# Two layers of experts on one core: another row of step numbers for the last layer-one job's routing

## The chip, the cores and the metric

The kernel runs on one core of a Trainium2 chip. The core has a matrix engine (TensorE, PE in the rows), a vector engine (VectorE, DVE), an activation engine (ScalarE, ACT), a general engine (GpSimd, POOL) and SyncE (SP); each runs its own queue of instructions in order, and semaphores tie the queues together. Sixteen DMA engines move data between memory and the core's buffers; DMAs are issued from the queues of SP, ACT and POOL. The metric is the device time of one execution in microseconds.

## The reference

Three stages follow one another. First, decayed linear attention over 2 x 768 tokens with 8 heads of 64. Its output, 1536 rows of 512, goes to a layer of 8 experts that takes one expert for each token, and the result of that to a second layer of 8 experts that takes two, chosen from logits with noise:

```python
x = attn_out ...reshape(B * S, H * D)          # 1536 x 512
# layer one
gate_w = softmax(normalised x @ expert_emb.T / tau)[argmax]
out[mask] = gate_w * (relu(x[mask] @ w1[e]) @ w2[e])
# layer two
noisy_logits = x @ w_gate + log1p(exp(x @ w_noise)) * noise
top2 = the two largest of noisy_logits, with softmax over the two
out[mask] += top2_w * (relu(x[mask] @ w1[e]) @ w2[e])
```

## The kernel before

The experts' work is cut into 18 jobs, numbered from 0. Jobs 0 to 7 are layer one, one expert each, with up to 224 rows of tokens. Jobs 8 and 9 are the first 256 rows of layer two's experts 0 and 1, job 10 is expert 2 of layer two with up to 416 rows, and jobs 11 to 17 are the rest of layer two. Jobs 8 and 9 run early: the rows of job 8 come from tokens of layer-one jobs 0 to 5, those of job 9 from jobs 0 to 6, those of job 10 from all.

A job has eight steps, one for each 128 columns of the hidden width. A step is: `hstep` (four products with the first weights, in a high and a low part, L751, L752, L756), `ystep` of two steps before (products with the second weights, L795 to L797 in jobs 8 and 9), whatever a table `todo` holds for this job and step, and `split`, which cuts the weights for the step three ahead into parts (ScalarE L348, L349; DVE L350, L352). The schedule is manual: each engine's queue holds its instructions in the order in which the program writes them.

For every layer-one job the result is routed to layer two by ten stages, put into `todo` during the next job. With the job they belong to named j, the numbers of a row such as `WHEN7` are the steps of job j + 1 at which the stages run; 8 and above are steps of job j + 2:

```python
stages = (pe_0, pe_1, post1_a, post1_b, post1_m, post1_h, post1_c, post1_c2, post1_d, post1_e)
when = {0: WHEN0, E - 3: WHEN5, E - 2: WHEN6, E - 1: WHEN7}
after = {E + i: when[E - 3 + i][-1] % NF for i in range(3)}
...
for n in range(NEARLY, E + 1):
    put(n + 1, after[n + 2], window2, n)
for j in range(E, NJ):
    put(j - 1, after.get(j, 0), gather2, j)
```

`pe_0` and `pe_1` make the layer's output rows and the gate products. `post1_a` is the gates' exponential and logarithm on ScalarE (L919, L921). `post1_b` finishes the noisy logits on DVE (L927, L928, and five small operations recorded at L331), `post1_m` finds the two largest and their numbers (L939, L941) and has POOL convert the numbers (L942) and subtract the two values (L943). `post1_h` makes the one-hot rows (DVE L950, POOL L954, L955) and the exponential of the difference (ScalarE L956). `post1_c` and `post1_c2` compute each token's rank in its expert (TensorE L963 to L966, DVE L972 to L987) and write the rows to memory (POOL L992). `post1_d` builds two factors of a table (DVE L999 to L1002), and `post1_e` multiplies them on TensorE (L1010) and adds the product to the table of layer two (DVE L1011).

A table gives a gather its indices: `window2` makes them on DVE (L658, L661), and `gather2` issues one indirect DMA on POOL for each 128 rows (L693). With `WHEN6`, whose last number is 12, the table for job 9 is done in job 8, step 4, and job 9's indices and gather follow in the same step. With `WHEN7` the same holds for job 10 in job 9. The transposes of gathered rows (L732) stand in job 8, step 6 for job 9 and in job 9, steps 6 and 7 for job 10. Results of job 8 go out through DVE L1054 and ScalarE L1052 and a scatter on POOL (L1056).

Within a step the functions run in the order in which they were put, with `post1_e`, `pe_0` and `pe_1` ahead of the others. The stages of the jobs were put ahead of `window2` and `gather2`.

In the profiled execution, steps 4 to 7 of job 8 begin on TensorE at 277.86, 280.90, 283.80 and 287.91 us, steps 0, 1, 6 and 7 of job 9 at 290.88, 293.77, 308.23 and 313.89 us, and job 10 at 319.63 us.

Of the kernel before, what the change touches and what calls it, by code (L numbers as in the profile page):

```python
# [59 lines left out]
WHEN = (2, 3, 3, 5, 6, 7, 9, 10, 11, 13)  # L60
WHEN5 = (2, 3, 3, 3, 5, 6, 7, 8, 9, 11)
WHEN6 = (2, 3, 5, 5, 7, 8, 9, 9, 11, 12)
WHEN7 = (2, 3, 4, 5, 5, 6, 7, 7, 7, 9)
ORDER2 = (0, 1, 2, 5, 3, 6, 4)
XG5 = (5, 6, 6, 4, 5)
XG6 = (6, 6, 6, 8, 8)
# [33 lines left out]
def emit(ctx, tc, qt, kt, k, v, lam, moe_expert_emb, moe_tau, moe_w1, moe_w2, moe2_w_gate, moe2_w_noise,  # L100
# [1094 lines left out]
# [3 lines that stand above are left out]
# [290 lines left out]
```

## Time and profile before

| | |
|---|---|
| median of 3 runs | 599.55 us (598.65 to 602.4) |
| profiled execution | 603.23 us, its span 601.5 us |
| TensorE busy | 577.0 us (96%) |
| DVE busy | 378.5 us (63%) |
| ScalarE busy | 293.6 us (49%) |
| POOL busy | 211.0 us (35%) |
| mean granted clock of TensorE | 0.98 |

The span runs from the first to the last instruction of one execution; the profiled execution's own time lies 1.7 us above it. Busy shares are over the whole span; which engine is late in a stage is read from the waits and the timeline of that stage. The granted clock is told as a share of 2.4 GHz; 0.50 is the lower level, 1.2 GHz.

### The profile page before, as it was taken

To read this page: it belongs to the slowest core of one execution; us is meant where nothing else is said; L and a number is where in the kernel's file an instruction comes from. 1 tells how busy PE (TensorE), PEld (TensorE's weight loads), DVE (VectorE), ACT (ScalarE), POOL (GpSimd) and SP (SyncE) were. 2 spreads that over 40 slices of the span, in tenths; PEclk is the share of its full clock that TensorE was granted. 3 is DMA by queue.
4 is the path that set the end of the run, shared out by engine and by line. 5 is a ranking of instruction groups with operands and counts; after the bars stand their busy time and mean duration, and the time that the engine had idled before them with its cause. 6 is when DMAs were issued, how large, how long until landed. Compare 5 with 4: busy or idle time off the path is not lost. (4 is left out here: it accounts for less than half of the span.)

```text
span 601.5 us, 11485 instructions
## 1 busy us (share of the span) xinstructions
PE 577.0 (96%) x4212; PEld 485.5 (81%) x4213; DVE 378.5 (63%) x1172; ACT 293.6 (49%) x689; POOL 211.0 (35%) x409
## 2 busy tenths in 40 slices
PE   6999989999999999999999999999999999999992
PEld 2899779999999998997767878788888898679761
DVE  3588858688888888888866455465664137324620
ACT  1366536677676766675544343434443135314410
POOL 5486634433524523223362401422303342412103
PEclk8699999999999999999999999999999999999997
DMA  6989737858777765856692734356526647747104
GB/s 204 340 300 373 285 94 253 313 194 282 279 282 266 273 222 189 303 177 198 201 316 103 229 141 145 52 196 171 153 56 160 210 98 235 239 142 192 18 5 57
DMA packets 59954, 119.51 MB, mean 199 GB/s; under 512 B 5469, under 2 KB 7045, under 8 KB 59890
## 3 DMA queue, kind: packets, MB, share of 16 engines
q10 hardware_dynamic: 37232, 73.74, 35.0%
q0 software_dynamic: 9376, 25.48, 16.3%
q1 hardware_dynamic: 13282, 19.48, 9.8%
q8 instruction: 35, 0.57, 0.4%
q14 instruction: 29, 0.24, 0.1%
HBM read 100.55 MB, written 18.14 MB: 197 GB/s over the span
## 5 line engine op out<-in xcount | busy, mean ns | idle before, releaser
L751 PE MATMUL h<-xs,h 128*128 128x224 f32 (+10 forms) x512 | 149.1, 314 | 0.0
L752 PE MATMUL h<-xs,h 128*128 128x224 f32 (+10 forms) x512 | 142.7, 302 | 0.0
L1056 POOL DMA_INDIRECT out_dram<-orow,ix x30 | 48.6, 1620 | 207.7 <-DVE orow L1054 153.4
L350 DVE TENSOR_TENSOR l<-r,h 128x512 bf16<-128x512 f32 x128 | 88.2, 689 | 33.4 <-ACT h L348 31.8
L787 ACT ACTIVATE hs<-h 128x224 fp32r<-128x224 f32 (+10 forms) x128 | 52.0, 406 | 103.4 <-PE h L756 103.0
L756 PEld LDWEIGHTS <-l 128*128 128x128 bf16 x896 | 74.1, 97 | 30.8 <-issue 8.5
L752 PEld LDWEIGHTS h<-xs,h 128*128 128x128 f32 x512 | 97.4, 190 | 1.5 <-DVE xs L737 0.5
L751 PEld LDWEIGHTS h<-xs,h 128*128 128x128 f32 x512 | 97.2, 190 | 1.3
L788 DVE SCALAR_TENSOR_TENSOR hs<-h,hs 128x224 fp32r<-128x224 f32 (+10 forms) x128 | 57.9, 452 | 51.8 <-ACT hs L787 51.5
L756 PE MATMUL h<-xs,l 128*128 128x224 bf16 (+10 forms) x512 | 87.9, 293 | 0.0
L352 DVE TENSOR_TENSOR l<-r,h 128x512 bf16<-128x512 f32 x125 | 85.5, 684 | 0.0
L348 ACT ACTIVATE h<-r 128x512 fp32r<-128x512 f32 x128 | 79.8, 623 | 5.7 <-DVE hs L788 1.9
L349 ACT ACTIVATE h<-r 128x512 fp32r<-128x512 f32 x128 | 79.5, 621 | 0.0
L749 PE MATMUL y<-hs,h 128*128 128x448 f32 (+5 forms) x256 | 64.2, 372 | 0.0
L756 PE MATMUL y<-hs,l 128*128 128x224 bf16 (+8 forms) x384 | 62.5, 284 | 0.0
L737 DVE TENSOR_TENSOR xs<-t,xs 128x416 fp32r<-128x416 f32 (+7 forms) x42 | 24.7, 590 | 55.5 <-ACT xs L736 55.2
L751 PE MATMUL y<-hs,h 128*128 128x416 f32 (+2 forms) x128 | 49.6, 388 | 0.0
L736 ACT ACTIVATE xs<-t 128x416 fp32r<-128x416 f32 (+7 forms) x42 | 21.6, 518 | 54.5 <-PE t L732 51.2
L797 PE MATMUL y<-h,hs 128*128 128x512 f32 x80 | 47.1, 589 | 0.0
L752 PE MATMUL y<-hs,h 128*128 128x416 f32 (+2 forms) x128 | 44.6, 349 | 0.0
L749 PEld LDWEIGHTS y<-hs,h 128*128 128x128 f32 x256 | 42.6, 189 | 0.9
L693 POOL DMA_INDIRECT xw<-x,g x28 | 31.9, 1141 | 18.2 <-PE h L756 7.5
(274 smaller groups left out, 924.5 us busy)
## 6 DMA issues: line engine op xcount, KB each, us to landing
r<-in_moe_w_dram ACTq DMA_DIRECT2D x66, 1024.0 KB, 7.1
r<-in_moe_w_dram SPq DMA_DIRECT2D x6, 1024.0 KB, 9.4
x<-row POOLq DMA_DIRECT2D x8, 517.0 KB, 8.0
out_dram<-zeros ACTq DMA_DIRECT2D x7, 512.0 KB, 6.1
qt<-in_qt_dram SPq DMA_DIRECT2D x12, 256.0 KB, 5.1
kr<-in_k_dram SPq DMA_DIRECT2D x12, 256.0 KB, 5.8
vt<-in_v_dram SPq DMA_DIRECT2D x12, 256.0 KB, 5.8
x<-xr POOLq DMA_DIRECT2D x11, 265.0 KB, 5.0
```

What stands on the lines that cost most here:

```text
L348: nc.scalar.activation(h1, a1, AF.Copy)
L349: nc.scalar.activation(h2, a2, AF.Copy)
L350: nc.vector.tensor_sub(l1, a1, h1.bitcast(FT))
L352: (nc.gpsimd if s < LEAD else nc.vector).tensor_sub(l2, a2, h2.bitcast(FT))
L749: nc.tensor.matmul(o[:, :2 * c], hi, mov, start=first, stop=last, skip_group_check=True)
L751: nc.tensor.matmul(o[:, :c], hi, mov[:, :c], start=first, stop=False, skip_group_check=True)
L752: nc.tensor.matmul(o[:, :c], hi, mov[:, c:], start=False, stop=last, skip_group_check=True)
L756: nc.tensor.matmul(o[:, :c], lo, upper_half(mov[:, :c]), start=first, stop=last, skip_group_check=True)
L787: nc.scalar.activation(hh, ph[:, :c], AF.Relu)
L788: nc.vector.scalar_tensor_tensor(hl, ph[:, :c], 0.0, hh.bitcast(FT), op0=OP.max, op1=OP.subtract)
L797: nc.tensor.matmul(PY[j][t], hl, h2, start=False, stop=f == NF - 1)
L1056: s = nc.gpsimd.indirect_dma_start(out=out[:, :], out_offset=bass.IndirectOffsetOnAxis(ap=ix[:p, t:t + 1], axis=0), in_=row[:p], in_offset ...
```

## The change

One row of step numbers changes, that for job 7, the last of layer one:

```diff
-WHEN7 = (2, 3, 4, 5, 5, 6, 7, 7, 7, 9)
+WHEN7 = (2, 3, 3, 4, 4, 5, 7, 7, 7, 8)
```

`post1_a` goes from step 4 to 3 of job 8, `post1_b` and `post1_m` from 5 to 4, `post1_h` from 6 to 5; `post1_c`, `post1_c2` and `post1_d` stay at step 7. `post1_e` goes from step 1 of job 9 to step 0, and by `after` the indices and the gather for job 10 go with it. The instructions are the same in number and kind; SP's queue does not change.

On DVE in job 8, step 4 (L1011 is the table's sum with job 6, `g` and `ok` are the indices and marks for job 9), the kernel before has:

```order
L1011 TENSOR_TENSOR tab_142<-tab_142,t 128x96
L658 TENSOR_SCALAR g_4705<-tab_142 128x2
L661 TENSOR_SCALAR ok_4706<-tab_142 128x2
L350 TENSOR_TENSOR l_4714<-r_4195,h_4712 128x512
L352 TENSOR_TENSOR l_4715<-r_4197,h_4713 128x512
L788 SCALAR_TENSOR_TENSOR hs<-h,hs 128x256
L927 RECIPROCAL q_4651<-q_4651 128x16
L928 SCALAR_TENSOR_TENSOR q_4651<-q_4651 128x16
```

and the changed kernel:

```order
L1011 TENSOR_TENSOR tab_142<-tab_142,t 128x96
L927 RECIPROCAL q_4651<-q_4651 128x16
L928 SCALAR_TENSOR_TENSOR q_4651<-q_4651 128x16
L331 TENSOR_TENSOR q_4651<-q_4651 128x16 x2
L331 TENSOR_TENSOR q_4651<-q_4651,lg_4650 128x16
L331 TENSOR_TENSOR q_4651<-q_4651,meta 128x16
L331 TENSOR_TENSOR q_4651<-q_4651,lg_4650 128x16
L939 MAX mx_4712<-q_4651 128x8 x2
L941 MAX_INDEX mi_4713<-mx_4712,q_4651 128x8 x2
L658 TENSOR_SCALAR g_4720<-tab_142 128x2
L661 TENSOR_SCALAR ok_4721<-tab_142 128x2
```

The indices for job 9 stand behind the eleven operations of job 7's decisions now; before, those came a step later.

On POOL in job 8, steps 4 and 5 (L693 is the gather for job 9):

```order
 L913 COPY row_4594<-meta 128x2
 L920 TENSOR_SCALAR q_4651<-q_4651 128x16
-L693 DMA xw<-x_69,g_4705 128x517 x2
-L942 CAST row_4594<-mi_4750 128x2x2
-L943 TENSOR_TENSOR q_4651<-mx_4749 128x2
-L954 TENSOR_TENSOR q_4651<-oh_4791 128x16
-L955 TENSOR_TENSOR ob_4794<-q_4651,ok_1352 128x16
+L942 CAST row_4594<-mi_4713 128x2x2
+L943 TENSOR_TENSOR q_4651<-mx_4712 128x2
+L693 DMA xw<-x_69,g_4720 128x517 x2
+L954 TENSOR_TENSOR q_4651<-oh_4757 128x16
+L955 TENSOR_TENSOR ob_4760<-q_4651,ok_1352 128x16
```

The gather for job 9 stands behind the conversion and the subtraction of job 7's decisions.

On POOL in job 9, steps 0 and 1 (L693 is the gather for job 10, L1056 a scatter of job 8's results):

```order
-L1056 DMA out_dram<-orow,ix 1952x512
-L693 DMA xw<-x_69,g_4953 128x517 x3
-L693 DMA xw<-x_69,g_4953 32x517
+L693 DMA xw<-x_69,g_4904 128x517 x3
+L693 DMA xw<-x_69,g_4904 32x517
+L1055 MEMSET spacer 1x1
+L1056 DMA out_dram<-orow,ix 1952x512
```

The gather for job 10 goes ahead of the scatters.

## Rows read from the trace of the kernel before

**Rows 1.** The page, part 1: busy us, share of the span, instructions.
```profile
PE 577.0 (96%) x4212; PEld 485.5 (81%) x4213; DVE 378.5 (63%) x1172; ACT 293.6 (49%) x689; POOL 211.0 (35%) x409
```

**Rows 2.** Waits of TensorE: us in total, times, longest us.
```profile
PE t L732 <- DMA xw<-x,g: 1.3, 4, 0.4
```

**Rows 3.** Timeline, TensorE, 311 to 320 us: start, duration, instruction, idle before.
```profile
311.53 0.30 PE L732 MATMUL t<-ident,xw 128*128 128x128 f32 x1 [0.35 <-DMA xw<-x,g]
...
312.81 1.16 PE L732 MATMUL t<-ident,xw 128*128 128x128 f32 x6 [0.36 <-DMA xw<-x,g]
...
313.89 0.39 PE L751 MATMUL h<-xs,h 128*128 128x256 f32 x1
...
318.38 1.32 PE L732 MATMUL t<-ident,xw 128*128 128x128 f32 x8
...
319.63 0.46 PE L751 MATMUL h<-xs,h 128*128 128x416 f32 x1
```

**Rows 4.** Windows: length, each engine's busy us, clock, DMA share, GB/s.
```profile
316.00:317.00 1.00, 1.00 (x5) 0.60 (x4) 0.62 (x2) 0.39 (x1) 1.00 (x1) 0.50 1.06 414
...
318.00:319.00 1.00, 1.00 (x8) 0.68 (x6) 0.00 (x0) 0.00 (x0) 0.45 (x2) 0.99 1.03 418
```

**Rows 5.** Timeline, POOL, 291 to 304 us.
```profile
291.97 0.81 POOL L992 DMA_DIRECT2D x<-row  x1 [0.30 <-POOL row L991]
...
298.56 1.68 POOL L1056 DMA_INDIRECT out_dram<-orow,ix  x1 [5.41 <-DVE tab L1011]
...
303.52 1.17 POOL L693 DMA_INDIRECT xw<-x,g  x1 [0.31 <-DVE ex L331]
```

**Rows 6.** DMA issues, us to landing: of 303 to 304.5, of 291 to 294.
```profile
xw<-x,g POOLq DMA_INDIRECT x1, 7.9
...
x<-row POOLq DMA_DIRECT2D x1, 517.0 KB, 4.6
```

**Rows 7.** Timeline, TensorE, 283 to 294 us (job 8, steps 6 and 7; job 9).
```profile
283.80 0.28 PE L751 MATMUL h<-xs,h 128*128 128x256 f32 x1
...
286.59 0.27 PE L732 MATMUL t<-ident,xw 128*128 128x128 f32 x1
...
287.18 0.98 PE L732 MATMUL t<-ident,xw 128*128 128x128 f32 x7 [0.31 <-DMA xw<-x,g]
...
287.91 0.37 PE L751 MATMUL h<-xs,h 128*128 128x256 f32 x1
...
293.77 0.28 PE L751 MATMUL h<-xs,h 128*128 128x256 f32 x1
```

**Rows 8.** Timeline, DVE, 281 to 294 us.
```profile
281.48 0.16 DVE L661 TENSOR_SCALAR ok<-tab 128x2 f32<-128x2 f32 x1
...
283.35 0.24 DVE L927 RECIPROCAL q<-q 128x16 f32<-128x16 f32 x1
...
285.13 0.16 DVE L941 FIND_INDEX8 mi<-mx,q 128x8 uint32<-128x8 f32 x1
...
293.17 0.56 DVE L1002 TENSOR_TENSOR pb<-oi,ge 128x384 f16<-128x384 f32 x1
```

**Rows 9.** Timeline, POOL, 281 to 287 us.
```profile
281.86 1.34 POOL L693 DMA_INDIRECT xw<-x,g  x1 [1.05 <-DVE ok L661]
...
283.50 0.97 POOL L693 DMA_INDIRECT xw<-x,g  x1 [0.30 <-issue]
...
285.89 0.64 POOL L943 TENSOR_TENSOR q<-mx 128x2 f32<-128x2 f32 x1
```

**Rows 10.** DMA issues, us to landing: of 283.4 to 284.6, of 313 to 314.2.
```profile
xw<-x,g POOLq DMA_INDIRECT x1, 3.6
...
xw<-x,g2r POOLq DMA_INDIRECT x1, 5.5
```

**Rows 11.** Timeline, ScalarE and its DMA queue, 280 to 286 us.
```profile
280.03 0.21 ACT L919 ACTIVATE q<-q 128x16 f32<-128x16 f32 x1
...
285.40 0.37 ACTq L320 DMA_DIRECT2D r<-in_moe_w_dram  x1
```

## The prediction, made before the changed kernel ran

> **What bounds the kernel now.** I read the page's busy shares first: TensorE is busy 577.0 of 601.5 us [rows 1], so a microsecond counts only if TensorE loses or wins it. The waits of TensorE come next. In the whole stretch that the change touches they hold one entry: the transposes of gathered rows, which waited four times for the gather's DMA, 1.3 us in all [rows 2]. The timeline says where. Three of the four waits stand in job 9, step 6, ahead of the transposes that feed job 10 [rows 3], and one in job 8, step 6, ahead of those that feed job 9 [rows 7]. Nothing else there is late by the profile, so the change can act only through these two gathers, and through what a wait does to TensorE's clock.
>
> The wait for job 10 is dearer than its own idle time. TensorE ended the work before it at 311.53 - 0.35 = 311.18 us and began the next step at 313.89 [rows 3], which is 2.71 us for eight transposes. Seven of them took 287.91 - 287.18 = 0.73 us in job 8 [rows 7], so eight take 0.83 and the wait cost 1.9 us. Then the granted clock fell to its lower level, 1.2 GHz (0.50 of 2.4 GHz), and was back at 0.99 in the slice from 318 us [rows 4]. In that time step 7 took 318.38 - 313.89 = 4.49 us [rows 3] against 286.59 - 283.80 = 2.79 us for a step with the same instructions in job 8 [rows 7], and the second eight transposes took 319.63 - 318.38 = 1.25 us against 0.83. The fallen clock cost 1.7 + 0.4 = 2.1 us. Wait and clock together are **4.0 us**, and this is all that an earlier gather for job 10 can win.
>
> **The change part by part.** No instruction is added or removed. Four things move.
>
> *The table and the gather for job 10 move from step 1 to step 0 of job 9.* The gather's indices are then ready one step, some 3 us, sooner. On POOL's queue the four gathers now stand ahead of the two scatters of job 8's rows. Before, the scatters went first, at 298.56 us, and the first gather was issued at 303.52 [rows 5]. It landed 7.9 us later [rows 6], after the time at which TensorE wanted it. In the changed order the gathers must wait for the rows of the last layer-one job, whose write is issued at 291.97 [rows 5] and lands 4.6 us later [rows 6], at 296.6. The indices follow the table's sum, which came just ahead of 298.56 [rows 5] and now comes a step of 2.8 us sooner, near 295.7. So the gathers start near 297, that is 6 us sooner. Even at 7.9 us the first lands at 305 and the last, some 4 us behind it, at 309. TensorE asks at 311.2: the wait goes, with 2 us to spare, and so does the fall of the clock. Term: **-4.0 us**, bounds -4.0 and 0 (the gathers stay late). What is late next there is the scatters, now issued some 4 us later; nobody waits for them before the next job's scatters. The four table products themselves come on TensorE at 293.77 [rows 7], just where their operand is finished (293.17 + 0.56 = 293.73 [rows 8]): 0 to 0.3 us, taken as 0.1 and left out of the sum.
>
> *The decisions of job 7 (reciprocal to the index search) move from step 5 to step 4 of job 8.* This is where it costs. Step 4 is also the step that builds job 9's indices and issues job 9's gather, and the order shows that the moved work stands ahead of both: on DVE eleven instructions between the table's sum and the indices, on POOL the cast and the subtraction (L942, L943) ahead of the two gathers. On DVE these eleven took from 283.35 to 285.13 + 0.16 = 285.29, 1.94 us [rows 8]. POOL's two need the result of the last of them and ended at 285.89 + 0.64 = 286.53 [rows 9], 1.24 us later; the indices (L658, L661) run beside these. Before, DVE began the indices just ahead of 281.48 [rows 8], at 281.4, and the gathers were issued at 281.86 and 283.50 [rows 9]. Now the first comes at 281.4 + 1.94 + 1.24 + 0.3 for the issue = 284.9 us. To that I add 0.4 us, because ScalarE's two small activations, 0.21 us the first [rows 11], also move a step up and delay the weight split on which DVE waits next: 285.3, that is 3.4 us late (3.0 without it). With the same spacing of 1.64 us the second gather is issued at 286.9.
>
> The second gather of job 9 landed 3.6 us after issue [rows 10], at 287.1, and TensorE already waited 0.31 us for it [rows 7]. There is no slack, so every microsecond is paid. The nearest row for a free queue gives 286.9 + 3.6 = 290.5, +3.4 us. But two weight blocks of 1 MB were issued at 285.40 [rows 11] and come some 0.8 us later in the changed order, so the gather now moves beside them. A gather that was issued into such a load took 5.5 us [rows 10]; one behind two scatters took 7.9 [rows 6]. I take 4.4, nearer to 3.6, since the load starts only about when this gather does: landing at 291.3. Term: **+4.2 us**, bounds +3.0 (no delay from ScalarE, 3.6 us) and 286.9 + 7.9 - 287.1 = +7.7.
>
> The Trainium skill, page "DMA: Bandwidth & Descriptors", section "Queues, rings and completion order", says that each DMA engine goes round the queues that have work, a packet from each in turn. By that rule the gather shares with the weight load and the term stays near +4.2; if it had to stand behind the whole load instead, the term would be near its upper bound. The 5.5 us of rows 10 lean to sharing.
>
> *TensorE's clock after that wait.* TensorE would stand idle, but for one transpose, from 286.59 + 0.27 = 286.9 to 291.3, 4.4 us. In the trace of before a wait spread over 311.18 to 313.89 brought the clock down [rows 3 to 4]; the longer one should too. There is one step, not a second set of transposes, in the slow stretch: **+1.7 us**, bounds 0 (no fall, as after the 0.31 us wait) and 2.6 (a slow stretch half as long again).
>
> *The one-hot rows (step 5) and the gates' exponential.* ScalarE's exponential L956 now waits about 2 us for POOL's late subtraction, with the splits for job 9's first step queued behind it; these are needed some 4 us later. DVE's share runs ahead of a TensorE that is itself late. Cost nothing; if that cover were gone, under 1 us. The ranks stay at step 7, so their chain keeps its place.
>
> **Sum:** -4.0 + 4.2 + 1.7 = +1.9 us. The profiled execution took 603.23 us, its span 601.5 and 1.7 around it, and would become 605.1. The runs shown have a median of 599.55, 3.7 us below that execution; the same addition gives **601.5 us**.
>
> **The rivals.** *A: as summed*, one wait exchanged for a somewhat dearer one, 601.5 us (its own range 599.5 to 604.0). Chance 0.62.
> *B: the wait moves but the clock holds.* Job 9's wait costs 3.0 to 4.2 us and no slow stretch follows: -1.0 to +0.2, about 599.2 us. For it: the one transpose in the middle of the wait, and the chance of where the fall lands. Against: the wait is longer than the one that brought a fall. Chance 0.20.
> *C: only the gain is seen,* -4.0, 595.5 us: the delayed gather is still in time. It needs a gather issued 3 us later to land no later; against it stands the 0.31 us that TensorE waits already. Chance 0.08.
> *D: the gather sinks in the weight load.* It lands at 294.8, +7.7, with the clock's 2.1, less 4.0: +5.8, 605.4 us. It decides from a landing time of about 7.5 us. For it: the 7.9 us row; against: that one stood behind scatters in its own queue. Chance 0.07.
> *E: the change does not do what it says* for job 10: the gathers, now ahead of the scatters, are held until the rows are written and land as late as before. Then +4.2 + 1.7 = +5.9, 605.5 us. Against: the write lands at 296.6 by its row, 14 us ahead of the need. Chance 0.03.
>
> **How the numbers follow.** A measurement of this kernel can tell about 1% from no change, that is 6.0 us: below 593.6 or above 605.5. Neither A, B nor C reaches these; D and E stand at the upper edge. Faster 0.01, slower 0.06, the same 0.93. The range takes in A and B with the bounds of the contention, and the 3.8 us over which the runs of before scatter: 597.0 to 605.0. It leaves out C and the ends of D and E.
>
> **What would show it.** In the changed trace: the first gather for job 9 issued 3.0 to 3.4 us later against the end of the preceding table sum, behind L943; a wait of 3 to 5 us at the transposes in job 8, step 6, and a stretch at 0.50 behind it; the gathers for job 10 ahead of the scatters; job 9, step 6 without a wait and step 7 at 2.8 us. The forecast is wrong if the wait in job 8 is under 2 us, if the clock falls in both places or in neither, or if a third wait turns up, at the table products of job 9, step 0.

## The result, and the profile after

The changed kernel takes 607.02 us (median of 4 runs, 605.68 to 609.43) against 599.63 us before (median of 4, 598.65 to 602.4): 7.4 us more by the medians, ratio 1.0106 with a 95% interval of 1.0075 to 1.0138, which is 4.5 to 8.3 us. The sum had given +1.9 us: the way is right, the size is a third to a quarter of the measured one, and the median lies outside the range. The two places and their signs are as forecast; the sizes of the two main terms are not.

The waits of TensorE in the changed kernel's profile (us in total, times, longest us) answer to [rows 2]:

```profile
PE t L732 <- DMA xw<-x,g: 5.6, 2, 4.5
...
PE y L795 <- DVE key L1142: 0.3, 1, 0.3
```

Four waits of 0.3 to 0.4 us became two, of 4.5 and 1.1 us, and a small new one came. The timeline of TensorE shows where; the first four lines answer to [rows 7], the last four to [rows 3]:

```profile
292.08 0.48 PE L732 MATMUL t<-ident,xw 128*128 128x128 f32 x1 [4.46 <-DMA xw<-x,g]
293.68 1.75 PE L732 MATMUL t<-ident,xw 128*128 128x128 f32 x7 [1.12 <-DMA xw<-x,g]
295.08 0.56 PE L751 MATMUL h<-xs,h 128*128 128x256 f32 x1
...
298.71 0.18 PE L963 MATMUL t<-oacc,ones 128*128 128x16 bf16 x1
...
319.43 1.32 PE L732 MATMUL t<-ident,xw 128*128 128x128 f32 x8
320.67 0.39 PE L751 MATMUL h<-xs,h 128*128 128x256 f32 x1
...
323.56 1.31 PE L732 MATMUL t<-ident,xw 128*128 128x128 f32 x8
324.81 0.46 PE L751 MATMUL h<-xs,h 128*128 128x416 f32 x1
```

Both waits now stand ahead of the transposes for job 9. Ahead of those for job 10 there is none: the eight run as one group, and the next step begins at once. TensorE's clock fell inside the wait, as the windows show (length, busy us of each engine, clock, DMA share, GB/s):

```profile
290.00:291.00 1.00, 0.00 (x0) 0.00 (x0) 0.00 (x0) 0.00 (x0) 0.00 (x0) 0.50 1.08 428
295.00:296.00 1.00, 1.00 (x7) 1.00 (x6) 0.69 (x1) 0.74 (x3) 0.00 (x0) 0.50 0.00 0
297.00:298.00 1.00, 1.00 (x8) 0.76 (x6) 1.00 (x3) 0.59 (x3) 0.00 (x0) 1.00 0.00 0
```

All of the engines but the DMA stand still at 290 us, and DMA moves 428 GB/s. What it moves is told by the queues. On DVE, the decisions of job 7 come first and the indices of job 9 behind them (compare [rows 8]):

```profile
282.30 0.24 DVE L927 RECIPROCAL q<-q 128x16 f32<-128x16 f32 x1
...
284.07 0.16 DVE L941 FIND_INDEX8 mi<-mx,q 128x8 uint32<-128x8 f32 x1
...
284.21 0.16 DVE L661 TENSOR_SCALAR ok<-tab 128x2 f32<-128x2 f32 x1
```

On POOL, the conversion and the subtraction, then the two gathers for job 9; the last two lines are the first gather for job 10 and the first scatter behind it (compare [rows 5, 9]):

```profile
284.30 1.32 POOL L942 CAST row<-mi 128x4 f32<-128x4 uint32 x1 [3.88 <-DVE g L658]
285.59 0.18 POOL L943 TENSOR_TENSOR q<-mx 128x2 f32<-128x2 f32 x1
285.93 1.09 POOL L693 DMA_INDIRECT xw<-x,g  x1 [0.16 <-DVE hs L788]
287.33 1.36 POOL L693 DMA_INDIRECT xw<-x,g  x1 [0.30 <-issue]
...
304.13 1.04 POOL L693 DMA_INDIRECT xw<-x,g  x1 [3.10 <-DVE ws L1034]
...
310.05 1.65 POOL L1056 DMA_INDIRECT out_dram<-orow,ix  x1 [0.23 <-issue]
```

The weight load on ScalarE's queue, two blocks of 1 MB, is issued between the two gathers, 286.26 - 284.65 = 1.6 us after the step's start as before (285.40 - 283.80 [rows 11]); the second block follows 0.4 us later. Its first line:

```profile
286.26 0.38 ACTq L320 DMA_DIRECT2D r<-in_moe_w_dram  x1
```

The two gathers took, from issue to landing, 6.1 and 6.3 us (6.0 to 6.6 in the later traces `a_again` and `decide_only`), where the second took 3.6 before [rows 10]:

```profile
xw<-x,g POOLq DMA_INDIRECT x1, 6.1
...
xw<-x,g POOLq DMA_INDIRECT x1, 6.3
```

To compare executions I use lengths of steps, from the first product of a step to the first of the next on TensorE's timeline. The time of a whole execution also holds the opening of the kernel, where the clock is not the same each time. The stretch from 18 to 20 us shows it, in the profiled execution of before and in one of the runs below, `table_only`, which has the same instructions there:

```profile
18.00:20.00 2.00, 1.66 (x24) 1.47 (x20) 0.45 (x2) 0.60 (x1) 1.98 (x2) 0.50 1.05 385
```

and in table_only:

```profile
18.00:20.00 2.00, 1.13 (x18) 1.14 (x20) 0.91 (x3) 1.19 (x4) 1.93 (x2) 0.98 1.06 389
```

Job 8, step 3 began at 272.85 us in the first and at 270.76 in the second: 2 us apart before anything of the change runs. Over all executions it began between 270.76 and 273.71 us. The steps in us, for all profiled executions of this study ("sum" is from job 8, step 3 to job 10; the steps not listed are the same in all, 10.9 us for 8.3 to 8.5 and 8.4 for 9.3 to 9.5; the last column is the ratio of times to before, with its interval):

| kernel | 8.6 | 8.7 | 9.0 to 9.2 | 9.6 | 9.7 | sum | ratio |
|---|---|---|---|---|---|---|---|
| before | 4.11 | 2.97 | 8.99 | 5.66 | 5.74 | 46.78 | 1 |
| b_again (before) | 4.11 | 2.98 | 9.01 | 5.30 | 4.13 | 44.87 | 1.0006 (0.9982 to 1.003) |
| b_third (before) | 3.93 | 2.96 | 9.01 | 5.39 | 4.16 | 44.79 | |
| b_fourth (before) | 4.02 | 2.98 | 9.01 | 5.32 | 4.16 | 44.83 | |
| after | 10.43 | 3.72 | 9.43 | 4.04 | 4.14 | 51.10 | 1.0106 (1.0075 to 1.0138) |
| a_again (after) | 10.75 | 4.57 | 9.42 | 4.03 | 4.13 | 52.21 | |
| table_only | 3.94 | 2.98 | 9.43 | 4.05 | 4.13 | 43.87 | 0.9978 (0.9954 to 1.0002) |
| decide_only | 10.42 | 4.49 | 8.98 | 5.24 | 4.14 | 52.57 | 1.0159 (1.011 to 1.0208) |
| gather_first | 3.96 | 2.96 | 9.43 | 4.05 | 4.14 | 43.88 | 0.997 (0.9945 to 0.9995) |
| load_late | 7.17 | 4.52 | 9.44 | 4.05 | 4.14 | 48.65 | 1.0078 (1.0051 to 1.0106) |
| pool_split | 6.63 | 4.55 | 9.44 | 4.05 | 4.13 | 48.14 | 1.0046 (1.0019 to 1.0073) |
| filled | 9.84 | 2.96 | 9.42 | 4.03 | 4.14 | 49.70 | 1.0085 (1.0056 to 1.0113) |

The usual sum of before is 44.8 us, that of after 51.1 to 52.2: 6.3 to 7.4 us. From the start of job 10 to the end of the span all twelve executions took 281.4 to 282.2 us, so no part of the difference lies behind job 10, and these 6.3 to 7.4 us are the measured difference within its interval.

### The profile page after: what moved, and what is told of

The parts are those of the page before. It is cut to its first block, busy times and chain, and to the rows that moved or that the text cites. A ratio compares the mean times of both kernels' runs of the same rounds, so it can differ in the third digit from the quotient of the medians.

```text
span 606.2 us, 11486 instructions
## 1 busy us (share of the span) xinstructions
PE 577.4 (95%) x4212; PEld 486.1 (80%) x4213; DVE 378.5 (62%) x1172; ACT 293.3 (48%) x689; POOL 212.7 (35%) x409
## 5 line engine op out<-in xcount | busy, mean ns | idle before, releaser
L1056 POOL DMA_INDIRECT out_dram<-orow,ix x30 | 47.6, 1587 | 205.0 <-DVE orow L1054 155.9
L693 POOL DMA_INDIRECT xw<-x,g x28 | 33.1, 1180 | 20.0 <-PE h L756 7.3
```

Source lines behind the costliest of these rows:

```text
L1056: s = nc.gpsimd.indirect_dma_start(out=out[:, :], out_offset=bass.IndirectOffsetOnAxis(ap=ix[:p, t:t + 1], axis=0), in_=row[:p], in_offset ...
```

## The experiments

My theory after the result: job 9's late gather, landing together with the weight load, is the loss, and what job 10 wins is small. The rivals: the first trace of before was untypical, so that there was nothing like 4 us to win; or the table's own move costs something.

**b_again, b_third, b_fourth.** The kernel before, unchanged.

> The kernel before, unchanged, for a second trace. Theory one (the loss is job 9's late gather; the wait for job 10's gather with the clock's fall, 3.2 us by the traces of before and after, is in the usual run of before): the trace shows TensorE waiting at the transposes of job 9, step 6, and a granted clock of 0.50 behind it, and a time near 599.6 us. Rival, the untypical trace (the profiled execution of before, 603.23 us, had that wait, the usual one of 599.6 us does not): no clock of 0.50 in job 9, step 7, and step 6 to job 10 about 3 us shorter than the 11.4 us of the first trace.

> The kernel before, a third trace, to see how often the clock falls behind job 10's wait. With the fall, job 9's steps 6 and 7 take 11.4 us and job 8, step 3 to job 10 takes 46.8 us; without it 9.4 and 44.9. Theory: the fall is not bound to the wait of 1 us, so that either may come.

> The kernel before, a fourth trace: as for the third, 46.8 or 44.9 us from job 8, step 3 to job 10.

The timeline of TensorE in b_again, ahead of job 10:

```profile
312.47 1.16 PE L732 MATMUL t<-ident,xw 128*128 128x128 f32 x6 [0.34 <-DMA xw<-x,g]
313.56 0.39 PE L751 MATMUL h<-xs,h 128*128 128x256 f32 x1
...
316.45 1.31 PE L732 MATMUL t<-ident,xw 128*128 128x128 f32 x8
```

A window of b_again behind that wait, in job 9, step 7:

```profile
315.00:316.00 1.00, 1.00 (x8) 0.56 (x6) 1.00 (x3) 0.60 (x2) 0.69 (x2) 1.00 1.03 389
```

The wait is there, the fall of the clock is not. In b_third and b_fourth steps 9.6 and 9.7 are as short. So three traces of four lack the fall that I read in the first [rows 4]. The theory holds for the wait, the rival for the clock. The wait was not quite the same: in the first trace TensorE stood idle for 1.0 us between 311 and 313 us, in the three others for 0.6 to 0.7 us in the same place.

**table_only** and **decide_only** each make half of the change:

```diff
 # table_only, against before
-WHEN7 = (2, 3, 4, 5, 5, 6, 7, 7, 7, 9)
+WHEN7 = (2, 3, 4, 5, 5, 6, 7, 7, 7, 8)
 # decide_only, against before
-WHEN7 = (2, 3, 4, 5, 5, 6, 7, 7, 7, 9)
+WHEN7 = (2, 3, 3, 4, 4, 5, 7, 7, 7, 9)
```

> Only the table's number of the last job goes from 9 to 8; the decisions stay where they were. Theory one: the wait and the clock's fall for job 10 go, job 9's gather keeps its place, 3.2 us less than before, about 596.4 us (ratio 0.995). Rival, the untypical trace: nothing to win, 599.6 us. Rival, a loss from the table step itself (the scatters behind the gathers, the products at job 9, step 0): above 601 us.

> Only the decisions move a step up (exponentials at 3, index search at 4, one-hot rows at 5); the table stays at 9. Theory one: job 9's gather is issued behind them and lands in the weight load; 6.3 us of wait and 0.75 us of slow clock more than before, with job 10's wait kept: about 606.7 us. Rival, a loss from the table step: 600 us, with the first part of it only.

The table's half gives 598.88 against 600.37 us, and its steps 9.6 and 9.7 are without a wait, 8.18 us instead of the usual 9.4 to 9.6. That is 1.2 to 1.4 us, of which 0.4 us is lost again in 9.0 to 9.2. The interval just includes no change, and the 3.2 us of the theory did not come. The half with the decisions gives 608.89 against 600.37 us, 2.2 us above what I expected for it, and its TensorE shows both waits of the changed kernel:

```profile
290.62 0.48 PE L732 MATMUL t<-ident,xw 128*128 128x128 f32 x1 [4.38 <-DMA xw<-x,g]
292.31 1.76 PE L732 MATMUL t<-ident,xw 128*128 128x128 f32 x7 [1.21 <-DMA xw<-x,g]
```

Job 9's wait, the large loss, belongs to the decisions alone.

**gather_first** is the changed kernel with the indices and the gather for job 9 put into the table of steps ahead of the stages:

```diff
+    put(E, after[E + 1], window2, E - 1)
+    put(E, after[E + 1], gather2, E + 1)
     for j in range(E):
         for f, fn in zip(GATES if j else GATES0, ...):
...
-    for n in range(NEARLY, E + 1):
+    for n in (NEARLY, E):
         put(n + 1, after[n + 2], window2, n)
     for j in range(E, NJ):
-        put(j - 1, after.get(j, 0), gather2, j)
+        if j != E + 1:
+            put(j - 1, after.get(j, 0), gather2, j)
```

> The changed kernel, but in job 8, step 4 the indices and the gather for job 9 stand ahead of the moved decisions, on DVE and on POOL. Theory one: the second gather is issued at its old place, the wait in job 8 shrinks to some 0.3 us, and what is left is the gain at job 10: about 596.4 us (ratio 0.995); by the rival of the untypical trace 599.6 us. If the order of these few instructions is not the cause, the time stays near 607 us.

598.37 against 600.37 us, again not the 596.4 of the theory. POOL's timeline has the second gather for job 9 3.2 us ahead of the transposes' turn:

```profile
281.71 0.97 POOL L693 DMA_INDIRECT xw<-x,g  x1 [0.30 <-issue]
```

TensorE's timeline has the eight transposes without a wait:

```profile
284.91 1.40 PE L732 MATMUL t<-ident,xw 128*128 128x128 f32 x8
...
286.07 0.36 PE L751 MATMUL h<-xs,h 128*128 128x256 f32 x1
```

The order of some dozen small instructions within one step is the cause. This version is 0.3% under before and 1.3% under the changed kernel (0.997 / 1.0106 = 0.987). It has the lowest median here, but table_only has the same steps (43.87 against 43.88 us): with the gather in its place, the earlier decisions themselves win nothing.

**load_late** moves one weight load from step 6 to step 7 of job 8; **pool_split** puts POOL's two operations behind the gather and leaves DVE's order as changed:

```diff
 # load_late, against the changed kernel
-        loads.setdefault(s, []).append(u)
+        loads.setdefault(s + (u == 20), []).append(u)
 # pool_split, against the changed kernel: L942 and L943 of job 7 run at the step's end
+        if j == E - 1:
+            held.append((pool_m, j, mx, mi))
...
+        for fn, *a in held:
+            fn(*a)
+        held.clear()
         split(s + LEAD)
```

> The changed kernel with one weight load, the two blocks that ScalarE's queue issues in job 8, step 6, put one step later. Nothing else moves. Theory (the late gather takes 6.1 to 6.3 us instead of 3.6 because it runs beside this load): the two gathers land 3.6 to 4 us after their issue, step 6 of job 8 falls from 10.4 to about 7.7 us, and the time is some 3 us under the changed kernel's. Rival (the gather is slow by itself, or by POOL's two operations ahead of it): landing and step 6 as in the changed kernel.

> The changed kernel, but POOL's conversion and subtraction stand behind the gather for job 9; DVE's order stays as changed, so that the gather is held only by DVE's eleven operations. The gathers are issued about 1.5 us sooner than in the changed kernel, some 2 us later than in the kernel before. Theory (the weight load decides): the first lands ahead of the load, the second after 4 to 5 us, step 6 of job 8 takes 6 to 7.5 us, the time is 3 to 4.5 us under the changed kernel's. Rival (each microsecond of issue counts as one, 6.1 us of landing throughout): step 6 takes 8.9 us, 1.5 us under.

In load_late POOL's timeline has the second gather at 284.89:

```profile
284.89 1.37 POOL L693 DMA_INDIRECT xw<-x,g  x1 [0.30 <-issue]
```

TensorE goes on with it 288.65 - 284.89 = 3.8 us later, against 293.68 - 287.33 = 6.4 us in the changed kernel:

```profile
286.97 0.33 PE L732 MATMUL t<-ident,xw 128*128 128x128 f32 x1 [1.78 <-DMA xw<-x,g]
288.65 1.11 PE L732 MATMUL t<-ident,xw 128*128 128x128 f32 x7 [1.35 <-DMA xw<-x,g]
289.40 0.56 PE L751 MATMUL h<-xs,h 128*128 128x256 f32 x1
```

A window of load_late, just after step 7 began:

```profile
290.00:291.00 1.00, 1.00 (x6) 1.00 (x6) 1.00 (x2) 1.00 (x3) 0.00 (x0) 0.50 0.00 0
```

With the load out of the way the same late gather costs 10.43 - 7.17 = 3.3 us less in step 6: 2.6 us of landing, as the theory had it, and 0.7 us in the transposes, which ran ahead of the clock's fall here. The clock takes back 0.8 of the 3.3: it falls just as the work resumes, and most of step 7 is slow (4.52 against 3.72 us). By the whole time load_late is 1.7 us under the changed kernel (1.0078 against 1.0106), with intervals that overlap; I had expected some 3 us. In pool_split the second gather is issued ahead of the load. POOL's timeline:

```profile
284.61 0.97 POOL L693 DMA_INDIRECT xw<-x,g  x1 [0.30 <-issue]
```

The load, on ScalarE's queue:

```profile
285.98 0.37 ACTq L320 DMA_DIRECT2D r<-in_moe_w_dram  x1
```

TensorE has the gather's rows 3.7 us after its issue:

```profile
286.74 0.33 PE L732 MATMUL t<-ident,xw 128*128 128x128 f32 x1 [1.34 <-DMA xw<-x,g]
288.33 0.98 PE L732 MATMUL t<-ident,xw 128*128 128x128 f32 x7 [1.27 <-DMA xw<-x,g]
```

Against the start of step 6 (282.44 us there, 284.65 in the changed kernel) this gather is issued at 284.61 - 282.44 = 2.17 instead of 287.33 - 284.65 = 2.68 us: half a microsecond sooner, not the 1.5 that I expected, for the first gather's issue took 1.94 us. Step 6 is 10.43 - 6.63 = 3.8 us shorter. That is not the price of the half microsecond alone, for the load moved too: it was issued 285.98 - 282.44 = 3.5 us after the step's start, where the changed kernel has 1.6. Against load_late, where the load is out of the way as well and the second gather is issued 284.89 - 282.23 = 2.66 us after the step's start, half a microsecond sooner makes step 6 shorter by 7.17 - 6.63 = 0.5 us. So without the load beside it the delay counts about one for one; the rest of the 3.8 us is the load and the clock. The rival's 6.1 us of landing throughout is out.

**filled** puts products ahead of the first transposes for job 9, so that TensorE is at work in the wait. The transposes overwrite what they write:

```diff
+        for _ in range(FILL if (j, b) == (E + 1, 0) else 0):
+            nc.tensor.matmul(pt, ones, warm, start=True, stop=True)
```

> The changed kernel with 20 extra products of zeros, 128x512 in bf16, ahead of the transposes for job 9, so that TensorE works through most of the wait; their result is overwritten. The wait for the gather stays. Theory: the clock stays at 1.00, the seven transposes after the wait take 0.7 instead of 1.4 us and step 7 takes 3.0 instead of 3.7 to 4.5: 1.5 to 2.2 us less than the changed kernel. Rival (the clock costs nothing, the wait is all): no difference.

TensorE's timeline of filled (its lines of code stand three lower):

```profile
284.78 4.49 PE L729 MATMUL t<-zeros,ones 128*128 128x512 bf16 x20
289.55 0.33 PE L735 MATMUL t<-ident,xw 128*128 128x128 f32 x1 [0.28 <-DMA xw<-x,g]
291.08 0.98 PE L735 MATMUL t<-ident,xw 128*128 128x128 f32 x7 [1.20 <-DMA xw<-x,g]
291.82 0.36 PE L754 MATMUL h<-xs,h 128*128 128x256 f32 x1
```

A window of filled that holds the second wait:

```profile
290.00:292.00 2.00, 0.92 (x8) 0.93 (x9) 0.00 (x0) 0.34 (x1) 0.00 (x0) 1.00 0.94 366
```

The clock stays at 1.00, the seven transposes take 0.74 us (1.40 in the changed kernel), step 7 takes 2.96, and the sum is 49.70 against 51.10 and 52.21: 1.4 to 2.5 us less, with the clock as the only thing changed in the two steps but for some tenths of landing time. By the whole time alone, 1.0085 against 1.0106, the two could not be told apart.

**a_again.** The changed kernel once more.

> The changed kernel, a second trace. Theory: job 8, step 6 takes 10.4 us again, since it is set by the gather that lands with the weight load; step 7 takes 3.6 to 4.5 us as the slow clock lasts into it; job 9's steps 6 and 7 take 8.2 us without a wait; job 8, step 3 to job 10 takes 51 to 52 us.

Step 8.6 takes 10.75 us, 8.7 takes 4.57 and the sum 52.21, each a little above what I expected; the waits for the gather are again two:

```profile
PE t L732 <- DMA xw<-x,g: 5.9, 2, 4.8
```

## Why the prediction was wrong

*That the change acts only through the two gathers and the clock:* right. Each half of the change, made alone, moves its own gather and the steps behind it.

*"Term: -4.0 us" for job 10: the step that failed most.* It read one execution as the usual one. Of the 2.1 us that it gave to the clock, three further traces of before show nothing (9.7 takes 4.13 to 4.16 us). The wait's 1.9 us had a second flaw: eight transposes of four tiles were priced at 0.83 us, from seven of two tiles, and they take 320.67 - 319.43 = 1.24. By the same flaw the 0.4 us of the second eight transposes was no cost of the clock even in the first trace: they took 1.25 us with the clock back at 0.99 [rows 4], and take 324.81 - 323.56 = 1.25 us in the changed kernel. The gain is 9.4 to 9.6 less 8.18, that is **1.2 to 1.4 us**. A hint stood in the times: the profiled execution took 3.7 us more than the median, and I carried the sum over to the median as if it held the same waits. With the gain put right and all else as forecast the sum would have been -1.3 + 4.2 + 1.7 = +4.6, or 604.2 us, still short of the measured time; the next term is needed for the rest.

*"Term: +4.2 us" for job 9, bounds +3.0 and +7.7:* the late issue was right, the landing mis-sized. The issue was late as worked out: against the step's start the second gather went out at 2.68 us instead of 283.50 - 283.80 = -0.3, 3.0 late (forecast 3.4). The landing was not 4.4 us but 6.3. I took the value nearer to the free queue, and expected the load 0.8 us later; it came no later against the step's start, 1.1 us ahead of the second gather. load_late shows that nearly the whole difference is the load. Step 8.6 grew by 10.43 - 4.0 = **6.4** and 10.75 - 4.0 = **6.7 us**; in the first of these 3.0 us is the later issue, 2.7 the longer landing, and 0.7 the transposes at the slow clock.

I weighed the rule of the Trainium skill, page "DMA: Bandwidth & Descriptors", section "Queues, rings and completion order", as sharing packet by packet. The trace of the changed kernel agrees where both are on the move, as the view of its DMA from 292.25 to 293 us shows (q0 is the gathers, q10 the load; packets, MB, share of the 16 engines):

```profile
q0 software_dynamic: 49, 0.20, 65.7%
q10 hardware_dynamic: 50, 0.10, 35.0%
```

But the time was lost before that. The first gather was issued at 285.93 us, and from 286 to 290.25 us the view has the load alone:

```profile
q10 hardware_dynamic: 450, 0.92, 65.2%
```

In load_late the first gather was issued at 283.50 us, and from 283.5 to 288.4 us both gathers were moved whole:

```profile
q0 software_dynamic: 160, 0.53, 37.3%
```

Beside the load the first packet of the gather came more than 4.3 us after its issue (as late in a_again and decide_only), without it less than 2. So the price is a late start of the gather behind a load that is under way, and not a small share of the bandwidth; my estimate had no such term. Why its packets start late no run here shows.

*"+1.7 us" for the clock behind the wait:* it fell, as forecast, and the size was about right. Step 8.7 grew by 0.75 and 1.6 us in the two traces of the changed kernel, 1.5 in decide_only; with the 0.7 us of the transposes, which the forecast had kept out of the slow stretch, it cost some 1.4 us or more by filled.

*The table products at job 9, step 0, "0 to 0.3":* a small loss came, two steps later. The table's sum and job 10's indices now run on DVE ahead of the scaling of job 8's rows (L1054), and TensorE, so I read it, needs that buffer of job 8's results free. The profile names the small DVE instruction right behind it (L1142), and no run takes the two apart. DVE of the changed kernel:

```profile
305.86 0.74 DVE L1054 TENSOR_SCALAR orow<-y,ws 128x512 f32<-128x512 f32 x1
```

TensorE, in job 9, step 2:

```profile
306.75 0.47 PE L795 MATMUL y<-h,hs 128*128 128x512 f32 x1 [0.32 <-DVE key L1142]
```

Steps 9.0 to 9.2 take 9.43 us instead of 9.0 wherever the table is early, in table_only and gather_first too: **+0.4 us** that the sum left out.

*The cover of the later operations:* right; ScalarE waited 2 us for POOL's subtraction and no step shows it.

Put together from the measured terms: -1.3 + 6.4 to 6.7 + 0.75 to 1.6 + 0.4 = 6.3 to 7.4 us, as the sums of the steps have it, and 4.5 to 8.3 by the ratio. Of the rivals, D, the gather that sinks in the weight load, is the nearest in its mechanism, with 605.4 us; but by its own sign, a landing time of about 7.5 us, it did not come: 6.0 to 6.6 us lies between its landing and that of A. E's 605.5 us is as near by chance: job 10's gathers did come early.

What stays open: when the clock falls behind a short wait. One of four traces of before has it, behind three waits of 0.28 to 0.36 us; the three others have two waits of that length and no fall. Whether the third wait made it, no run here says.

## What to carry to other kernels

A step number in a table says when a function is called, not what it stands ahead of: where two chains share a step, put the one that ends in a DMA first. A gather's landing time depends on what is issued beside it, so a delay of issue has a price with a jump in it, at the point where it meets the next load: here the 3.0 us of delay cost 3.0 us, and the load 2.7 us on top. Before a wait of one traced execution is booked as a gain, its time is held against the median: an execution well above it may hold the very stall that the sum wants to remove.

## What the runs showed of the hardware

The same gather of 128 rows took 3.6 us from issue to landing on quiet queues (before, the second for job 9) and 6.1 to 6.3 us in the changed kernel, where a load of two 1 MB blocks was issued 0.3 us behind the first gather and 1.1 us ahead of the second; its packets began to move only after some 3 us of the load. TensorE's granted clock fell to 0.50 behind the waits for job 10, 1.0 us in all, in one execution of before, and stayed at 1.00 behind 0.6 to 0.7 us of such waits in three; in load_late it fell only when the work had resumed. In the kernel's first 30 us the clock differs from run to run, and the start of job 8, step 3 lies up to 3 us apart (270.76 to 273.71) among traces with the same instructions there: more than the whole gain of the best version.
